# One pool of SBUF slots for raw and split expert weights in a fused attention, MLP and top-1 expert kernel

## The chip, the cores and the metric

The kernel runs on one core of a Trainium2 chip. The metric is the device time of one execution in microseconds: the median of the runs of the kernel before is 708.6 us (three runs, 708.15 to 708.81).

## What is computed

The input is `q`, `k`, `v` of shape (4, 8, 576, 64). Three stages follow each other on 2304 tokens of 512 values:

```python
# 1 attention in a window: query i sees keys i-63 .. i
attn = softmax(where(0 <= i - j < 64, q @ k.T / 8, -1e9)) @ v
# 2 MLP, float64 weights (512 x 2048 and 2048 x 512)
x = relu(attn @ w_in) ** 2 @ w_out
# 3 eight experts, top-1, only for tokens with x @ w_skip > 0
e = argmax(x @ w_gate); gate = softmax(x @ w_gate)[e]
out = x + gate * (relu(x @ w1[e]) @ w2[e])     # w1: 512 x 1024, w2: 1024 x 512
```

All matmuls are float32 in accuracy. Stages 2 and 3 get it by splitting each operand into a rounded high part ("hi", type fp32r) and the rest ("lo"), and adding three products: hi*hi, hi*lo and lo*hi.

## The kernel before

Tokens are worked on in nine chunks of 256 (18 tiles of 128). The MLP walks `units`, pairs of a chunk and one of eight blocks of 256 hidden columns: `l1` (line 428) computes a block's hidden values, `l2` (line 448) two units later adds its part of the output. Attention of the next chunk, the routing of the last one and the preparation of weights are put between them by `inject` (line 596). After the last chunk comes a stage written in a fixed order (from line 705), in which the last two tiles are routed, and then the experts, also in fixed order (from line 872).

An expert takes its tokens in tiles of 128. `static(e, xt)` (line 851) does the first tile of expert e in straight code, `extras(e, ...)` (line 837) the second and further ones, under run-time conditions (lines 839, 842, 844) that every engine tests for itself and jumps over when they are false. In these data expert 0 has two tiles, expert 2 three, every other one at most one, so the order of work is static 0, extra 0, static 1, two extras of 2, static 2, 3, 4, 5, 6, 7, with a jump over the extras between static 2 and 3, 3 and 4, and so on. `ex_block` (line 764) is one tile: 24 matmuls `l1e` (line 774; three passes of four for each half of the hidden columns: x hi with w hi, x hi with w lo, x lo with w hi), relu on ScalarE (779), four transposes (784) and a split into hi (788, ScalarE) and lo (789, VectorE) for each half, 24 matmuls `l2e` (799), the gated sum (821, VectorE) and an indirect store (823, GpSimd). The input of the next block is transposed and split in the middle of it (lines 757 to 762, 672, 673).

The weights of an expert are eight pieces of 128 x 1024 floats (512 KB), four of w1 and four of w2. `ew_start` (line 470) loads a piece on the SyncE queue into one of eight raw buffers: `r0` to `r3` of a pool `wx`, or half of one of the two buffers `xt`, which the MLP has left. It starts nothing when eight pieces are raw. `ew_split` (line 492) turns the oldest raw piece into hi and lo, in tags `s0` to `s31` of the pool `wp`; the MLP's weights lay there before. Piece m of an expert always takes the same two tags, alternating between two sets of sixteen, one for even and one for odd experts. hi is a copy on ScalarE (504), except for piece (2, 2) of experts 2 to 7, which VectorE copies (502). lo is a subtraction on VectorE (506), except for piece (2, 3) of experts 2 to 7, which GpSimd does.

When this happens is written by hand: `ew_plan` (line 590) for the last chunk (fifteen loads, eleven splits), `EWS` (line 41) for the fixed stage (three loads), then `FILLS` (line 49), which gives for six places in a static block the number of splits of the next expert and of loads: 8 and 8 in all. Eight loads stand between extra 0 and expert 1. Each queue works in order, so a load that waits for its buffer holds back the loads behind it.

Of the kernel before, what the change touches and what calls it, by code (L numbers as in the profile page):

```python
# [8 lines left out]
F32 = mybir.dt.float32  # L9
F32R = mybir.dt.float32r  # L10
# [9 lines left out]
P = 128  # L20
B, H, S, D = 4, 8, 576, 64
NTOK = B * S
DM = H * D
NT = NTOK // P
CT = 2
NCH = NT // CT
# [4 lines left out]
NJ = DFF // 256  # L31
NE = 8
POOL_LO = ((2, 3),)
SPLIT_V = 5
DVE_HI = ((2, 2),)
PRO = [int(c) for c in '0010101010']
QK_H = (0, 1)
WARM = 10
NST = 3
LOADN = 3  # L40
EWS = (3, 0, 0)
LATE = (0,)
KEEP = (14, 20, 12, 12)
LOOK = 5
# [1 line left out]
DOT0 = 1  # L46
DOT00 = 6
ROW = NE * NT
FILLS = ((2, 2), (1, 1), (1, 1), (2, 2), (2, 2), (0, 0))
TAIL = 3  # L50
FE = 1024
KF = FE // P
# [9 lines left out]
def body(ctx, tc, qt_d, kt_d, vw_d, wi_d, wo_d, w9_d, w9r_d, w1_d, w2_d, out):  # L62
    nc = tc.nc
# [7 lines left out]
    wp = pool("wp", 1)  # L71
# [92 lines left out]
        if t != 3 * CT - 1 and n < NT:  # L164
            load(n)

    wi_t, wo_t = {}, {}
    raw_q = []
    conv_n = [0]

# [23 lines left out]
    def conv_next():  # L194
        if not raw_q:
            return
        raw, tag, kind, j, half = raw_q.pop(0)
        hw, lw = raw[:, :, 1], raw[:, :, 0]
        f = st.tile([P, 512], I32, tag="f", name="f")
        ff = f.bitcast(F32)  # L200
        hf = hw.bitcast(F32)
        nc.scalar.activation(out=hf, in_=hf, func=AF.Copy, scale=F64_SCALE)
        nc.gpsimd.tensor_scalar(
            out=hf, in0=hf, scalar1=F64_MAX, scalar2=-F64_MAX, op0=ALU.min, op1=ALU.max)
        nc.vector.tensor_scalar(
            out=f, in0=hw, scalar1=3, scalar2=None, op0=ALU.logical_shift_left)
        nc.vector.scalar_tensor_tensor(
            out=f, in0=hw, scalar=SIGN, in1=f, op0=ALU.bitwise_and, op1=ALU.bitwise_or)
        nc.vector.scalar_tensor_tensor(
            out=f, in0=lw, scalar=29, in1=f,  # L210
            op0=ALU.logical_shift_right, op1=ALU.bitwise_or)
        w = wp.tile([P, 2, 512], F32R, tag=tag, name=f"w{kind}{j}_{half}")
        (wi_t if kind == "i" else wo_t)[j, half] = w
        nc.scalar.copy(out=w[:, 0, :], in_=ff)  # L214
        conv_load(nc.gpsimd.tensor_tensor(
            out=w[:, 1, :], in0=ff, in1=w[:, 0, :].bitcast(F32), op=ALU.subtract))
# [125 lines left out]
    def rt_logits(t):  # L342
        xT = x2T_t.pop(t)
        pl = psa()
        for k in range(KD):
            nc.tensor.matmul(
                pl[:, 0:10], lhsT=xT[:, k * P:(k + 1) * P], rhs=w9[:, k, :],
                start=(k == 0), stop=(k == KD - 1))
        lg = small.tile([P, 10], F32, tag="lg", name="lg")
        nc.vector.tensor_copy(out=lg, in_=pl[:, 0:10])  # L350
        rt_argmax(t, lg)
# [110 lines left out]
            x2_evac(c * CT + 1, acc_t[c][1], 1)  # L462

    w1_t, w2_t = {}, {}
    ew_load, ew_raw = [], []
    ew_pool = []

    pair = []

    def ew_start():  # L470
        if not ew_load:
            return
        kind, e, i = ew_load[0]
        if len(ew_raw) > (6 if kind == 2 and i % 2 == 0 else 7):
            return
        ew_load.pop(0)
        r = (8 * e + 4 * (kind - 1) + i) % 8
        if r < 4:
            raw = ew_pool[0].tile([P, 1024], F32, tag=f"r{r}", name=f"r{kind}_{e}_{i}")
        else:  # L480
            if r % 2 == 0:
                pair.append(xtp.tile([P, 2, 1024], F32, tag="xt", name=f"r{kind}_{e}_{i}"))
            raw = pair[-1][:, r % 2, :]
        if kind == 1:
            nc.sync.dma_start(out=raw, in_=w1_d[e, i * P:(i + 1) * P, :])
        else:
            nc.sync.dma_start(  # L487
                out=raw.rearrange("p (a b) -> p a b", b=DM),
                in_=w2_d[e, i * 2 * P:(i + 1) * 2 * P, :].rearrange("(k p) n -> p k n", p=P))
        ew_raw.append((kind, e, i, raw))  # L490

    def ew_split():
        if not ew_raw:
            return
        kind, e, i, raw = ew_raw.pop(0)
        m = 2 * ((8 * e + 4 * (kind - 1) + i) % (2 * NJ))
        hi, lo = [
            wp.tile([P, 1024], F32R, tag=f"s{m + h}", name=f"e{kind}_{e}_{i}_{h}")
            for h in range(2)]
        (w1_t if kind == 1 else w2_t)[e, i] = (hi, lo)  # L500
        if (kind, i) in DVE_HI and e > 1:
            nc.vector.tensor_copy(out=hi, in_=raw)  # L502
        else:
            nc.scalar.copy(out=hi, in_=raw)  # L504
        eng = nc.gpsimd if (kind, i) in POOL_LO and e > 1 else nc.vector
        eng.tensor_tensor(out=lo, in0=raw, in1=hi.bitcast(F32), op=ALU.subtract)  # L506

    def grp_ops(c):
        grp = [(c * CT + i, g) for i in range(CT) for g in range(2)]
# [42 lines left out]
    if True:  # L552
# [34 lines left out]
            for _ in range(PRO[s]):  # L587
                conv_next()

        ew_plan = {(0, 0): 4, (1, 0): 1}  # L590
        for j in range(2, NJ - 1):
            ew_plan[j, 1] = 2

        def inject(u, s):
            for op in slots.pop((u, s), ()):
                op()
            for _ in range(2 if u < 2 else 1):
                conv_next()
            v = u - first[NCH - 1]
            for _ in range(ew_plan.get((v, s), 0)):  # L600
                ew_start()
            for _ in range(ew_plan.get((v - 1, s), 0) if v <= SPLIT_V else 0):
                ew_split()

        n_u = len(units)
        for u in range(n_u):
            if u == first[2]:
                assert not raw_q
                st_stack.close()
                (w9p,), st_stack = scoped(("w9p", 1, {}))  # L610
                w9b = w9p.tile([P, NE + 1, DM], F32, name="w9b")
                nc.sync.dma_start(
                    out=w9b, in_=w9r_d.unsqueeze(0).to_broadcast([P, NE + 1, DM]))
                w9b_t.append(w9b)
            if u == last[1] + LAG + 2:
                ps_s_stack.close()
                ps_a.append(pool("ps_a2", 2, space=PSUM))
            if u == first[NCH - 1]:
                st_stack.close()
                kv_stack.close()  # L620
                (wx, gx), st_stack = scoped(("wx", 1, {}), ("gx", 1, {}))
                ew_pool.append(wx)
                for e in range(NE):
                    ew_load += [(1, e, i) for i in range(4)] + [(2, e, i) for i in range(4)]
            if u < n_u:
                l1(*units[u])
                inject(u, 0)
            if u >= LAG:
                c, j = units[u - LAG]
                if c < NCH - 1 or j < NJ - TAIL:  # L630
                    l2(c, j)
                inject(u, 1)
        c, ta, tb = NCH - 1, NT - 2, NT - 1
        tabs = gx.tile([P, ROW, 2], I32, name="tabs")
# [70 lines left out]
        with tc.manual_schedule():  # L705
# [3 lines left out]
            xa = x2_t[ta]  # L709
            xT0 = ps_acc.tile([P, DM], F32, tag="acc0", name="xT0")  # L710
            l2(c, NJ - TAIL, (1,))
            for _ in range(EWS[0]):
                ew_start()
            rt_tr(ta, 1)
            for j in range(NJ - TAIL + 1, NJ - 1):
                l2(c, j, (1,))
            rt_logits(ta)
            place(xT0, early, ident, True)
            for _ in range(EWS[1]):
                ew_start()  # L720
            l2(c, NJ - 1, (1,), (0,))
            pa = rank_mm(ta)
            sela = slot_of(ta, pa)
            rt_rank(ta, pa)
            rt_scatter(ta)
            l2(c, NJ - 1, (1,), (1,))
            x2_evac(tb, acc_t[c][1], 2)
            xb = x2_t[tb]
            pick_mm(0, sela)
# [21 lines left out]
            nc.vector.tensor_scalar(  # L751
                out=cnt, in0=cnt, scalar1=7, scalar2=None, op0=ALU.logical_shift_right)
            nc.scalar.dma_start(out=tabs, in_=tab_v)
            for _ in range(EWS[2]):
                ew_start()

        def ex_x(tx, inner=True):
            xg = tx[2]
# [91 lines left out]

        def static(e, xt):
            def fill(i):
                n, m = FILLS[i]
                if i == LOADN and e + 1 < NE:
                    for x in range(e + (e > 0), e + 2):
                        load_n(x)
                for _ in range(n):
                    if ew_raw and ew_raw[0][1] <= e + 1:
                        ew_split()
                for _ in range(m if e > 0 else 0):  # L860
                    ew_start()

            if e + 2 < NE:
                t0[e + 2] = fetch(e + 2, 0, 0, e + 2)
            if e + 2 < NE:
                t1[e + 2] = fetch(e + 2, 1, 1, e + 2)
            return ex_block(
                e, t0[e], xt, fill,
                (lambda: ex_x(t0[e + 1], False)) if e + 1 < NE else (lambda: None),
                e in LATE)  # L870

        with tc.manual_schedule():
            t0[1] = fetch(1, 0, 0, 1)
            t1[0] = fetch(0, 1, 1, 0)
            t1[1] = fetch(1, 1, 1, 1)
            xt = static(0, xt)
            extras(0, t1[0])
            for _ in range(8):
                ew_start()
            for e in range(1, NE):  # L880
                extras(e, t1[e])
                xt = static(e, xt)
# [46 lines left out]
```

## Time and profile before

| | |
|---|---|
| median of the runs | 708.6 us |
| span of the profiled execution | 705.2 us; what lies around it isn't listed apart, the three runs lie 3.0 to 3.6 us above the span |
| attention and MLP | to about 541 us |
| static 0 and extra 0 | about 541 to 568 us |
| static 1, two extras of expert 2 | 569.2 to 609.4 us |
| static 2 to 7, ending with the stores | 609.8 to 705.2 us |
| busy share | TensorE 94%, VectorE 69%, ScalarE 44%, GpSimd 23% |

The page of the profile gives the busy share of each engine in 40 equal slices of the span (17.6 us each), and the groups of instructions that cost most. Further views were asked of the trace: which wait of an engine was ended by what, the instructions in order of time, the busy time in chosen stretches with the granted clock of TensorE (1.00 is 2.4 GHz), and all the records of one source line. A wait that ended by "issue" is one for which the trace shows no other engine and no transfer.

### The profile page before, as it was taken

What the parts mean: (1) busy time and instruction counts of PE and PEld (TensorE: products, weight loads), DVE (VectorE), ACT (ScalarE), POOL (GpSimd) and SP (SyncE); (2) the same over time, 40 slices, a digit from 0 to 9 for tenths busy, and PEclk for the clock granted to TensorE, in tenths of its full rate; (3) what the DMA queues carried; (4) which work ended last, traced back from release to release, by engine and by line L of the source; (5) the groups of instructions that cost most, each with busy time, mean ns of one, the idle gap of its engine ahead of it and who ended that gap; (6) DMA issues with size and microseconds to landing.
All of it is one profiled execution on the core that took longest, in us unless ns stands there. A gap on an engine that the chain in (4) does not pass through costs nothing. (4 is left out here: it accounts for less than half of the span.)

```text
span 705.2 us, 12314 instructions
## 1 busy us (share of the span) xinstructions
PE 659.6 (94%) x4461; PEld 571.9 (81%) x4461; DVE 486.3 (69%) x1354; ACT 307.8 (44%) x729; POOL 160.0 (23%) x181
## 2 busy tenths in 40 slices
PE   6699798899999999999999999999999898998786
PEld 4588687679998989989989989889988676776564
DVE  5989999967937836935945945954755363399871
ACT  4775535443434424334334334344442352476541
POOL 5556555510100000000000000030011432226420
PEclk9889999999999999999999999999999999999998
DMA  8964543344123123022122121116335644288820
GB/s 288 265 214 140 166 128 122 113 127 166 35 66 98 38 61 98 31 68 78 51 68 78 51 68 66 62 61 238 122 115 190 218 153 141 73 287 323 284 72 8
DMA packets 51076, 88.70 MB, mean 126 GB/s; under 512 B 24046, under 2 KB 24302, under 8 KB 50864
## 3 DMA queue, kind: packets, MB, share of 16 engines
q1 hardware_dynamic: 47584, 83.38, 35.6%
q0 software_dynamic: 2976, 3.95, 1.7%
q8 instruction: 46, 0.75, 0.4%
q10 hardware_dynamic: 432, 0.32, 0.1%
q14 instruction: 38, 0.31, 0.1%
HBM read 79.07 MB, written 12.49 MB: 130 GB/s over the span
## 5 line engine op out<-in xcount | busy, mean ns | idle before, releaser
L424 PE MATMUL h<-xt,wi 128*128 128x256 f32 x576 | 166.5, 290 | 5.1 <-ACT r L437 3.1
L426 PE MATMUL h<-xt,wi 128*128 128x256 f32 x576 | 165.1, 288 | 0.0
L425 PE MATMUL h<-xt,wi 128*128 128x256 f32 x576 | 164.4, 287 | 0.0
L424 PEld LDWEIGHTS h<-xt,wi 128*128 128x128 f32 x576 | 111.4, 193 | 9.5 <-ACT r L437 4.1
L424 PE MATMUL acc<-wo,gh 128*128 128x512 f32 x288 | 115.7, 406 | 2.5 <-ACT wo L214 2.5
L426 PE MATMUL acc<-wo,gl 128*128 128x512 f32 x288 | 112.7, 393 | 1.4 <-DVE gl L445 1.4
L425 PE MATMUL acc<-wo,gh 128*128 128x512 f32 x288 | 113.6, 394 | 0.0
L425 PEld LDWEIGHTS h<-xt,wi 128*128 128x128 f32 x576 | 111.5, 194 | 2.5
L426 PEld LDWEIGHTS h<-xt,wi 128*128 128x128 f32 x576 | 111.5, 194 | 0.4
L444 DVE TENSOR_TENSOR r<-r 128x512 f32<-128x512 f32 x72 | 53.5, 744 | 62.2 <-ACT gh L443 62.0
L437 ACT ACTIVATE r<-h 128x512 f32<-128x512 f32 x72 | 42.3, 593 | 115.6 <-PE h L426 113.3
L506 DVE TENSOR_TENSOR e<-r,e 128x1024 fp32r<-128x1024 f32 x58 | 73.3, 1283 | 28.0 <-ACT e L504 21.5
L416 POOL DMA_INDIRECT tab_d<-route,posi x18 | 19.5, 1086 | 314.7 <-DVE mx L356 182.5
L335 DVE CUSTOM_DVE_ANT_0 prod<-sm,w9b 128x512 f32<-128x512 f32 x108 | 74.1, 686 | 0.2
L504 ACT CAST e<-r 128x1024 fp32r<-128x1024 f32 x58 | 59.6, 1050 | 27.6 <-PE h L426 14.4
L263 ACT ACTIVATE sm<-sm,nmx 128x128 f32<-128x128 f32 x144 | 56.1, 392 | 26.6 <-DVE nmx L257 25.1
L426 PEld LDWEIGHTS acc<-wo,gl 128*128 128x128 f32 x288 | 54.1, 188 | 13.4 <-DVE gl L445 2.1
L424 PEld LDWEIGHTS acc<-wo,gh 128*128 128x128 f32 x288 | 54.0, 189 | 12.4 <-ACT wo L214 3.4
L774 PE MATMUL h<-e,xh 128*128 128x512 f32 x176 | 49.4, 410 | 13.0 <-issue 6.6
L425 PEld LDWEIGHTS acc<-wo,gh 128*128 128x128 f32 x288 | 54.4, 189 | 8.4
L445 DVE TENSOR_TENSOR gl<-r,gh 128x512 fp32r<-128x512 f32 x72 | 53.3, 741 | 1.9
L774 PEld LDWEIGHTS h<-e,xh 128*128 128x128 f32 x176 | 31.9, 191 | 23.3 <-issue 14.9
(158 smaller groups left out, 1065.0 us busy)
## 6 DMA issues: line engine op xcount, KB each, us to landing
r<-in_w_dram SPq DMA_DIRECT2D x64, 512.0 KB, 5.4
v<-in_vw_dram SPq DMA_DIRECT2D x18, 512.0 KB, 3.6
ri<-in_wi_dram SPq DMA_DIRECT2D x16, 512.0 KB, 4.0
ro<-in_wo_dram SPq DMA_DIRECT2D x16, 512.0 KB, 3.5
k<-in_kt_dram SPq DMA_DIRECT2D x18, 384.0 KB, 3.9
qpad<-in_qt_dram SPq DMA_DIRECT2D x36, 128.0 KB, 3.2
x_d<-sm SPq DMA_DIRECT2D x17, 256.0 KB, 2.6
out_dram<-sm SPq DMA_DIRECT2D x17, 256.0 KB, 3.0
```

The costliest lines, as they stand in the source:

```text
L263: nc.scalar.activation(out=e[:, u, :], in_=e[:, u, :], func=AF.Exp, bias=nmx[:, u:u + 1], scale=-1.0, accum_out=sums[:, u:u + 1])
L335: nc.vector.tensor_tensor_reduce(out=prod, in0=x2_t[t], in1=w9b_t[0][:, j, :], scale=1.0, scalar=0.0, op0=ALU.mult, op1=ALU.add, accum_out ...
L416: nc.gpsimd.indirect_dma_start(out=tab_d, out_offset=bass.IndirectOffsetOnAxis(ap=posi, axis=0), in_=route[:, t, :], in_offset=None, bound ...
L424: nc.tensor.matmul(out_ap, lhsT=ah, rhs=bh, start=start, stop=False)
L425: nc.tensor.matmul(out_ap, lhsT=ah, rhs=bl, start=False, stop=False)
L426: nc.tensor.matmul(out_ap, lhsT=al, rhs=bh, start=False, stop=stop)
L437: nc.scalar.activation(out=r, in_=hp.rearrange("p a b -> p (a b)"), func=AF.Relu)
L444: nc.vector.tensor_tensor(out=r, in0=r, in1=r, op=ALU.mult)
L445: nc.vector.tensor_tensor(out=glf, in0=r, in1=ghf.bitcast(F32), op=ALU.subtract)
L504: nc.scalar.copy(out=hi, in_=raw)
L506: eng.tensor_tensor(out=lo, in0=raw, in1=hi.bitcast(F32), op=ALU.subtract)
L774: nc.tensor.matmul(hp[f], lhsT=xt[a][:, k * P:(k + 1) * P], rhs=w1_t[e, k][b][:, f * 512:(f + 1) * 512], start=(i == 0), stop=(i == len(m1 ...
```

## The change

The two kinds of buffers become one list, `slot_q`, of 40 slots of 128 x 1024 floats: the 32 tags `s0` to `s31`, `r0` to `r3`, and four halves of `xt`. A load takes the first slot of the list (not a half of `xt`, which holds fp32r only), a split takes two and gives back that of its raw piece, and `ew_free` gives back an expert's w1 slots at the fourth place of its static block and its w2 slots at the sixth. `ew_pump(keep)` issues loads as long as more than `keep` slots are free. The MLP's weight tags join the list as the last chunk has used them. `DVE_HI` is empty, so that ScalarE makes every hi. In the last chunk eight pieces are split instead of eleven; static 0 then splits eight where before it split five.

```diff
-SPLIT_V = 5
-DVE_HI = ((2, 2),)
+EWV = (0, 0, 2, 2, 2, 2)
+DVE_HI = ()
-EWS = (3, 0, 0)
-FILLS = ((2, 2), (1, 1), (1, 1), (2, 2), (2, 2), (0, 0))
+FILLS = ((2, 3), (1, 2), (1, 0), (2, 3), (2, 0), (0, 5))
...
-    def ew_start():
...
+    ew_load, ew_raw, slot_q, w_slot = [], [], [], {}
+
+    def slot(dt):
+        n = next(n for n, q in enumerate(slot_q) if dt is F32R or isinstance(q, tuple))
+        q = slot_q.pop(n)
+        if isinstance(q, tuple):
+            return q[0].tile([P, 1024], dt, tag=q[1], name=f"e_{q[1]}"), q
+        return q, q
+
+    def slot_pair():
+        pr = xtp.tile([P, 2, 1024], F32R, tag="xt", name="e_xt")
+        slot_q.extend([pr[:, 0, :], pr[:, 1, :]])
+
+    def ew_pump(keep):
+        while ew_load and len(slot_q) > keep:
+            kind, e, i = ew_load.pop(0)
+            raw, q = slot(F32)
...
+            ew_raw.append((kind, e, i, raw, q))
 
     def ew_split():
...
-        kind, e, i, raw = ew_raw.pop(0)
-        m = 2 * ((8 * e + 4 * (kind - 1) + i) % (2 * NJ))
-        hi, lo = [
-            wp.tile([P, 1024], F32R, tag=f"s{m + h}", name=f"e{kind}_{e}_{i}_{h}")
-            for h in range(2)]
+        kind, e, i, raw, q = ew_raw.pop(0)
+        (hi, qh), (lo, ql) = slot(F32R), slot(F32R)
         (w1_t if kind == 1 else w2_t)[e, i] = (hi, lo)
+        w_slot[kind, e, i] = (qh, ql)
...
         eng.tensor_tensor(out=lo, in0=raw, in1=hi.bitcast(F32), op=ALU.subtract)
+        slot_q.append(q)
+
+    def ew_free(kind, e):
+        for i in range(4):
+            slot_q.extend(w_slot[kind, e, i])
...
             v = u - first[NCH - 1]
-            for _ in range(ew_plan.get((v, s), 0)):
-                ew_start()
-            for _ in range(ew_plan.get((v - 1, s), 0) if v <= SPLIT_V else 0):
-                ew_split()
+            if v >= 0 and s == 1:
+                for _ in range(EWV[v] if v < len(EWV) else 0):
+                    ew_split()
+                ew_pump(3 if v < NJ else NE + 1)
...
             def fill(i):
-                n, m = FILLS[i]
+                n, keep = FILLS[i]
+                if e > 0 and i == 3:
+                    ew_free(1, e)
+                if e > 0 and i == 5:
+                    ew_free(2, e)
...
-                for _ in range(m if e > 0 else 0):
-                    ew_start()
+                if e > 0:
+                    ew_pump(keep)
...
             extras(0, t1[0])
-            for _ in range(8):
-                ew_start()
+            ew_free(1, 0)
+            ew_free(2, 0)
+            ew_pump(5)
```

In the fixed stage the three loads of `EWS` are replaced by `ew_pump(NE + 1)` at four places.

## Rows read from the trace of the kernel before

**Rows 1.** The page: busy share of the DMA engines, 40 slices of 17.6 us.
```profile
DMA  8964543344123123022122121116335644288820
```
**Rows 2.** Waits of TensorE, 609 to 690 us: total, times, longest.
```profile
PE h L774 <- issue: 7.3, 4, 2.8
PE h L774 <- PEq L839: 2.3, 1, 2.3
PE h L774 <- PEq L844: 0.4, 1, 0.4
```
**Rows 3.** TensorE in order of time (start, us): static 1 and 3 to 7.
```profile
569.16 2.08 PE L774 MATMUL h<-e,xh 128*128 128x512 f32 x8 [1.03 <-PEq L839]
...
625.88 0.73 PE L774 MATMUL h<-e,xl 128*128 128x512 f32 x2 [0.73 <-issue]
...
636.45 1.84 PE L774 MATMUL h<-e,xh 128*128 128x512 f32 x7
639.58 0.50 PE L774 MATMUL h<-e,xh 128*128 128x512 f32 x1 [1.29 <-issue]
...
650.85 1.16 PE L774 MATMUL h<-e,xh 128*128 128x512 f32 x4
654.44 1.20 PE L774 MATMUL h<-e,xh 128*128 128x512 f32 x4 [2.44 <-issue]
...
666.40 0.47 PE L774 MATMUL h<-e,xh 128*128 128x512 f32 x1
669.70 2.66 PE L774 MATMUL h<-e,xh 128*128 128x512 f32 x7 [2.83 <-issue]
672.16 1.91 PE L774 MATMUL h<-e,xl 128*128 128x512 f32 x4
...
686.06 2.08 PE L774 MATMUL h<-e,xh 128*128 128x512 f32 x8 [2.30 <-PEq L839]
```
**Rows 4.** TensorE's jump at line 839 after static 2 to 6: ns, start us.
```profile
L839 PEldq COMPARE_BRANCH  x1: 343/343/343, 620.7 to 620.7; - x1
...
L839 PEldq COMPARE_BRANCH  x1: 320/320/320, 634.6 to 634.6; - x1
...
L839 PEldq COMPARE_BRANCH  x1: 322/322/322, 648.9 to 648.9; - x1
...
L839 PEldq COMPARE_BRANCH  x1: 313/313/313, 664.5 to 664.5; - x1
...
L839 PEldq COMPARE_BRANCH  x1: 3884/3884/3884, 682.0 to 682.0; - x1
```
**Rows 5.** Stretches: PE, PEld, DVE, ACT, POOL busy (count), clock, DMA share, GB/s.
```profile
632.00:636.00 4.00, 4.00 (x21) 3.26 (x19) 3.96 (x6) 3.89 (x6) 0.97 (x1) 1.00 1.02 413
...
670.00:680.00 10.00, 10.00 (x44) 7.86 (x43) 6.34 (x6) 5.55 (x8) 2.07 (x1) 0.83 0.37 121
...
678.00:682.00 4.00, 4.00 (x22) 3.33 (x22) 3.71 (x5) 3.81 (x6) 0.10 (x1) 1.00 0.01 2
```
**Rows 6.** Casts and a split, groups by line, 609 to 690 us: busy us, mean ns.
```profile
L504 ACT CAST e<-r 128x1024 fp32r<-128x1024 f32 x33 | 33.8, 1051 | 0.4
...
L506 POOL TENSOR_TENSOR e<-r,e 128x1024 fp32r<-128x1024 f32 x5 | 12.1, 2424 | 15.3 <-ACTq L839 15.2
...
L502 DVE CAST e<-r 128x1024 fp32r<-128x1024 f32 x5 | 9.1, 1827 | 0.0
```
**Rows 7.** Expert 0: loads on SyncE, and the transpose for extra 0.
```profile
546.59 4.50 SPq L487 DMA_DIRECT2D r<-in_w_dram  x4
...
554.46 0.66 PE L761 MATMUL a<-ident,xg 128*128 128x128 f32 x4 [1.15 <-DMA xg<-x_d,tabs]
```
**Rows 8.** All gathers of line 648, issue to landing.
```profile
DMA to landing us min/median/max: 3.6/6.1/6.9
```
**Rows 9.** The waits of ScalarE, 553 to 705 us: the one cast at static 1.
```profile
ACT e L504 <- PEq L842: 4.0, 1, 4.0
```
**Rows 10.** The page, DMA issues: a weight piece, KB, us from issue to landing.
```profile
r<-in_w_dram SPq DMA_DIRECT2D x64, 512.0 KB, 5.4
```

More of the change, by code (lines that the diff above doesn't have):

```diff
@@ L165, in load_next @@
             load(n)
-    wi_t, wo_t = {}, {}
+    wi_t, wo_t, w_tag = {}, {}, {}
     raw_q = []
@@ L211, in conv_next @@
             op0=ALU.logical_shift_right, op1=ALU.bitwise_or)
+        w_tag[kind, j, half] = tag
         w = wp.tile([P, 2, 512], F32R, tag=tag, name=f"w{kind}{j}_{half}")
@@ L464, in body @@
     w1_t, w2_t = {}, {}
-    ew_load, ew_raw = [], []
-    ew_pool = []
-    pair = []
-    def ew_start():
[L471 to L490, printed above, removed]
+    ew_load, ew_raw, slot_q, w_slot = [], [], [], {}
[12 more added lines that the diff above has]
+            raw, q = slot(F32)
+            if kind == 1:
+                nc.sync.dma_start(out=raw, in_=w1_d[e, i * P:(i + 1) * P, :])
+            else:
+                nc.sync.dma_start(
+                    out=raw.rearrange("p (a b) -> p a b", b=DM),
+                    in_=w2_d[e, i * 2 * P:(i + 1) * 2 * P, :].rearrange("(k p) n -> p k n", p=P))
+            ew_raw.append((kind, e, i, raw, q))
     def ew_split():
@@ L588, in body, with w_free @@
                 conv_next()
-        ew_plan = {(0, 0): 4, (1, 0): 1}
-        for j in range(2, NJ - 1):
-            ew_plan[j, 1] = 2
+        def w_free(kind, j):
+            slot_q.extend((wp, w_tag[kind, j, h]) for h in range(2))
         def inject(u, s):
@@ L621, in body @@
                 (wx, gx), st_stack = scoped(("wx", 1, {}), ("gx", 1, {}))
-                ew_pool.append(wx)
+                slot_q.extend((wx, f"r{i}") for i in range(4))
                 for e in range(NE):
@@ L626, in body @@
                 l1(*units[u])
+                c, j = units[u]
+                if c == NCH - 1:
+                    if j == 0:
+                        slot_pair()
+                    w_free("i", j)
+                    if j == NJ - 1:
+                        slot_pair()
                 inject(u, 0)
@@ L631, in body @@
                     l2(c, j)
+                    if c == NCH - 1:
+                        w_free("o", j)
                 inject(u, 1)
@@ L711, in body @@
             l2(c, NJ - TAIL, (1,))
-            for _ in range(EWS[0]):
-                ew_start()
+            w_free("o", NJ - TAIL)
+            ew_pump(NE + 1)
             rt_tr(ta, 1)
@@ L716, in body @@
                 l2(c, j, (1,))
+                w_free("o", j)
             rt_logits(ta)
             place(xT0, early, ident, True)
-            for _ in range(EWS[1]):
-                ew_start()
+            ew_pump(NE + 1)
             l2(c, NJ - 1, (1,), (0,))
@@ L726, in body @@
             l2(c, NJ - 1, (1,), (1,))
+            w_free("o", NJ - 1)
             x2_evac(tb, acc_t[c][1], 2)
@@ L753, in body @@
             nc.scalar.dma_start(out=tabs, in_=tab_v)
-            for _ in range(EWS[2]):
-                ew_start()
+            ew_pump(NE + 1)
         def ex_x(tx, inner=True):
@@ L859, in fill @@
                         ew_split()
-                for _ in range(m if e > 0 else 0):
-                    ew_start()
+                if e > 0:
+                    ew_pump(keep)
             if e + 2 < NE:
@@ L877, in body @@
             extras(0, t1[0])
-            for _ in range(8):
-                ew_start()
+            ew_free(1, 0)
+            ew_free(2, 0)
+            ew_pump(5)
             for e in range(1, NE):
```

## The prediction, made before the changed kernel was built or run

> **What bounds the kernel now.** I read the waits of TensorE first. For the last chunk of the MLP that view is empty, and from 609 to 690 us, six straight expert blocks, its only waits are three kinds that name no other engine and no transfer: 7.3 us ended by "issue" and 2.3 and 0.4 us at a jump [rows 2]. VectorE, ScalarE and the weight loads end none of them. So a lighter VectorE or an earlier load is worth nothing there by itself, and the question is what the 10 us are.
>
> The order of TensorE's work tells [rows 3]. The 2.83 us stop in static 6 comes after one matmul of the block, that of static 5 after four, that of static 4 after seven, that of static 3 after ten (the eight x-hi ones and two of the four x-lo ones), and static 7 can't start at all for 2.30 us. The data those matmuls want differ from case to case; a place that slides by exactly three matmuls per expert is a place in the program. TensorE stops where its instructions end and the next stretch of them has to be brought in after the jump over the extras. The jump itself shows it once: after static 6 it takes 3884 ns, otherwise 313 to 343 [rows 4].
>
> From the jump to the first matmul after the stop, or to the jump's own end for static 7, I get 625.88-620.7 = 5.2 us, 639.58-634.6 = 5.0, 654.44-648.9 = 5.5, 669.70-664.5 = 5.2 and 3.9 us [rows 3, 4]. The four slow ones have weight loads in flight: at the jump of 634.6 the DMA engines are full, 413 GB/s; at that of 682.0 their share is 0.01 [rows 5]. So I read the time as 3.9 us alone and 5.0 to 5.5 beside loads. This is the one way in which the change can reach TensorE in this stage. After the longest stop the clock fell, too: 0.83 granted from 670 to 680, between the 1.2 and 2.4 GHz levels [rows 5]; seven matmuls took 2.66 us and four 1.91, where in static 4 and 5 they took 1.84 and 1.16 [rows 3]. That cost 0.82 + 0.75 = 1.6 us.
>
> **The change, part by part.**
>
> *Casts.* Six copies leave VectorE (the five of the window: 9.1 us, 1.83 each, since a GpSimd subtraction of 2.4 us stands beside most) and ScalarE gets six of 1.05 us [rows 6]. None is behind a wait of TensorE: 0. The new ones run at the end of a block behind ScalarE's other casts; its next urgent work is a relu some 3 us into the following block. Their price with the cover gone would be 1.05 us for each of six blocks, 6 us; their gain is at most zero, as no wait ends on VectorE.
>
> The Trainium skill, "SBUF — State Buffer", section "SBUF: two separate sides", says that VectorE and GpSimd lock each other out of a shared port for a whole instruction, also when VectorE only subtracts two SBUF operands. By that rule the subtraction that remains would still wait for GpSimd, and the removed copies would return only their bare time. The sum is zero by either.
>
> *Loads.* Counting the list through by hand: at the end of the last chunk fifteen pieces are raw or on their way, where before eight were the limit. Nothing is then issued until extra 0 is over, except one piece late in static 0. Twelve come after extra 0, and in static 1 to 4 eight per block: one at the third place, three at the fourth, one at the fifth, three at the sixth. None is left for static 5 and 6. Before, the engines are still at 0.8 in the slices up to 670 us [rows 1]. So the last jumps find no load: static 6 falls from 5.2 to 3.9, -1.3 us. Ahead of the jumps after static 2 to 4 I estimate the loads of the third and fourth place to be issued some 3 us before the jump and, at 5.4 us to land [rows 10], to be in flight for 2 us behind it; those of the fifth and sixth wait for GpSimd's subtraction and for TensorE's end of the block, and come after the fetch. I take half of the time as loaded, 4.6 us: -0.6 of 0.73, -0.4 of 1.29, -0.9 of 2.44 [rows 3]. Bounds: nothing (the instructions come as late as before), and 3.9 everywhere, -0.7, -1.1, -1.6 and -1.3. I take -3.2 in all, 0 to -4.7.
>
> *Clock.* The stop of static 6 then falls to 1.5 us. Stops of 2.44 and 2.30 were not followed by a lower clock in their blocks, that of 2.83 was [rows 3, 5]: -1.6, bounds 0 and -1.6.
>
> *Expert 0.* The transpose for extra 0 waits 1.15 us for its gather, and four loads are issued beside it [rows 7]. Gathers land in 3.6 to 6.9 us [rows 8], and these two stood near the upper end. Without the loads I expect them in time: -1.15. But static 0 splits eight pieces where it split five, and one more cast, 1.05 us [rows 6], stands ahead of ScalarE's copy (line 788) that the second half of the output needs; I estimate that 0.4 of it shows. Sum -0.75, bounds -1.15 and +1.05.
>
> *Expert 1.* Here the change adds. Before, ScalarE's first cast of static 1 waits for the end of extra 0 at TensorE [rows 9], because a buffer used under a condition counts as busy to the end of it. The freed slots of expert 0 are of that kind, so eleven loads start at once at 568 us, on a stretch whose first slices had almost none [rows 1]. Continuing the slide of three matmuls, static 1 meets the end of its instructions after sixteen, 3.7 us after 569.16, and no stop is seen there now. Brought in 1.3 us later it would stop by up to 1.3; I take +0.65, bounds 0 and +2.6 (the jump before it late as well).
>
> *Waits added.* A split now writes into slots just freed. ScalarE's cast at the third place takes the raw slot of the second split of the first place, so it must wait for VectorE's subtraction on it, and ScalarE's relu and TensorE's transposes stand behind. VectorE's two subtractions start after the jump and may be held by GpSimd's 2.4 us [rows 6]. I estimate they end 4.7 us into a block that has no stop, the cast is due at 5.0: 0, at worst 0.7 in each of three blocks. A load that waits for its slot holds only loads on SyncE. SyncE's stores of the MLP's output and its table load come before the crowded part.
>
> Sum: -3.2 - 1.6 - 0.75 + 0.65 = -4.9 on a span of 705.2. The runs lie 3.4 us above that span, and I carry this over: 708.6 - 4.9 = 703.7.
>
> **The rivals.**
>
> *The stops stay (chance 0.21, 708.3).* The place of a jump alone would set the stops, and loads would not. For it: the 3.9 us comes from a jump whose own target was missing, the others from the stretch behind a target, so load is not the only difference between them [rows 4]. Against it: the four with traffic all took over 5 us, and the one without is the shortest. The gather's -0.75 and expert 1 would leave 708 to 709. The Trainium skill, "Runtime: NRT & Kernel Launch", section "Instruction fetch mechanics", states that a taken branch out of the two pages held forces a fetch before execution goes on; that the jump of 3884 ns agrees with. It says nothing of loads beside it, which is this rival.
>
> *The program moves (slower; 711, chance 0.11, and 0.07 the other way, 699).* If TensorE's program ahead of the experts gets longer, every jump lands nearer to the end of its stretch; each matmul less is 0.23 us more (eight took 2.08, one 0.47: 1.61 over seven) in each of static 3 to 5 [rows 3]. At five matmuls the gain is used up: three blocks x 5 x 0.23 = 3.5, and about 1.3 more in static 2 and 6. At seven it is 2 to 3 us slower, 711. TensorE's waits before the experts would need a dozen extra instructions. Against: the change moves none of its matmuls, and waits on weights were covered by later ones. Shorter by as much removes nearly all stops but the last, 699.
>
> *Expert 1 and the new waits take it back (slower; 710, chance 0.07).* +2.6 at static 1 and 0.7 in three blocks is 4.7 against the forecast, and with the clock not recovered 1.6 more. It decides when VectorE's second subtraction of the first place ends later than 5 us into the block.
>
> *Loads too deep or too late* would show as casts waiting for a transfer; with sixteen to nineteen pieces ahead of the split I give it none.
>
> **How the numbers follow.** Forecast 703.7, own range 701 to 706.5, chance 0.54. Rivals: 0.21 stays, 0.11 and 0.07 program moved, 0.07 expert 1 and waits. The range reaches from 700.5 (all fetches at 3.9 us, clock, 1.15: 7.5 us less, 701.1, and a little of the shorter program) to 709.8, leaving out 0.2. What a measurement can tell from no change is 0.2%, 1.4 us. Faster: the forecast, the shorter program and some of the first rival, 0.63; the same: most of the first rival, 0.17; slower: 0.20.
>
> **What would show it.** Right: jumps at the same ten, seven, four, one, none matmuls, with 4.6 and 3.9 us to the next matmul; clock 1.00 from 670 to 680; no loads after about 655; no wait of the transpose for extra 0. Wrong: other places of the stops, 5 us beside idle DMA engines, a stop in static 1 over 1.3 us, or TensorE waiting for ScalarE's relu behind a cast.

## The result, and the profile of the changed kernel

The kernel after takes 713.67 us (median of 4 runs, 712.64 to 714.46), the kernel before 708.38 us beside it: the ratio is 1.0072, 95% interval 1.0054 to 1.0089. The change makes the kernel slower by 5.3 us; the forecast was 4.9 us faster, and 713.7 lies above the range.

The profiled execution of the kernel after has a span of 711.9 us and a time of 713.56 us, so 1.7 us lie around a span. That of the kernel before, with a span of 705.2 us, thus ran some 1.5 us below its median, and the two profiles are 6.7 us apart where the medians are 5.3 apart. The ledger below is that of the profiles.

The waits of TensorE, 609 to 700 us, answer to [rows 2], with the last jump in it too: the kinds are the same, and "issue" has grown from 7.3 to 9.3 us.

```profile
PE h L783 <- issue: 9.3, 4, 3.5
PE h L783 <- PEq L848: 2.2, 2, 2.0
PE h L783 <- PEq L853: 0.4, 1, 0.4
```

TensorE in order of time, static 3 to 7 (as [rows 3]; line 774 is now 783):

```profile
622.80 2.08 PE L783 MATMUL h<-e_s,xh 128*128 128x512 f32 x8
...
627.22 0.99 PE L783 MATMUL h<-e_s,xl 128*128 128x512 f32 x2 [1.89 <-issue]
...
639.28 0.47 PE L783 MATMUL h<-e_xt,xh 128*128 128x512 f32 x1 [0.15 <-PEq L848]
...
643.67 0.50 PE L783 MATMUL h<-e_s,xh 128*128 128x512 f32 x1 [2.55 <-issue]
...
661.13 0.50 PE L783 MATMUL h<-e_xt,xh 128*128 128x512 f32 x1 [3.54 <-issue]
...
676.70 1.88 PE L783 MATMUL h<-e_s,xh 128*128 128x512 f32 x7 [1.29 <-issue]
...
691.21 2.78 PE L783 MATMUL h<-e_s,xh 128*128 128x512 f32 x8 [2.04 <-PEq L848]
```

The jumps that go with them (as [rows 4]; line 839 is now 848), ns and start:

```profile
L848 PEldq COMPARE_BRANCH  x1: 342/342/342, 620.9 to 620.9; - x1
...
L848 PEldq COMPARE_BRANCH  x1: 320/320/320, 637.4 to 637.4; - x1
...
L848 PEldq COMPARE_BRANCH  x1: 323/323/323, 654.5 to 654.5; - x1
...
L848 PEldq COMPARE_BRANCH  x1: 313/313/313, 673.0 to 673.0; - x1
...
L848 PEldq COMPARE_BRANCH  x1: 3624/3624/3624, 687.4 to 687.4; - x1
```

The stops stand at the same five places, but their sizes are others: 1.89, 2.55, 3.54, 1.29 and 2.04 us where [rows 3] had 0.73, 1.29, 2.44, 2.83 and 2.30. From the jump to the next matmul it takes 627.22-620.9 = 6.3, 643.67-637.4 = 6.3, 661.13-654.5 = 6.6 and 676.70-673.0 = 3.7 us, and the last jump itself 3.6. Before, the first three were 5.2, 5.0 and 5.5.

The weight loads on SyncE (start, length, count) around these jumps:

```profile
617.68 0.33 SPq L483 DMA_DIRECT2D e_r<-in_w_dram  x1
619.04 1.41 SPq L485 DMA_DIRECT2D e_s<-in_w_dram  x3
...
633.62 0.33 SPq L483 DMA_DIRECT2D e_s<-in_w_dram  x1
634.63 1.41 SPq L485 DMA_DIRECT2D e_s<-in_w_dram  x3
...
650.85 0.33 SPq L483 DMA_DIRECT2D e_r<-in_w_dram  x1
651.86 0.39 SPq L485 DMA_DIRECT2D e_s<-in_w_dram  x1
652.30 0.46 SPq L485 DMA_DIRECT2D e_r<-in_w_dram  x1
652.85 0.42 SPq L485 DMA_DIRECT2D e_s<-in_w_dram  x1
658.72 0.37 SPq L485 DMA_DIRECT2D e_r<-in_w_dram  x1
```

Four pieces are issued in the last 3.2 to 3.8 us ahead of each of the first three jumps, none of them in the last 0.8 us, and none is issued after 659. In the kernel before, one piece was issued 3.3 us ahead of each of these jumps, and two only 0.6 and 0.2 us ahead:

```profile
620.11 0.90 SPq L487 DMA_DIRECT2D r<-in_w_dram  x2
...
633.92 0.90 SPq L487 DMA_DIRECT2D r<-in_w_dram  x2
...
648.31 0.90 SPq L487 DMA_DIRECT2D r<-in_w_dram  x2
```

Stretches with TensorE's busy time, granted clock, DMA share and GB/s (as [rows 5]):

```profile
620.00:630.00 10.00, 7.96 (x30) 0.88 0.80 266
640.00:650.00 10.00, 7.45 (x28) 0.83 0.88 316
...
654.50:658.80 4.30, 2.94 (x12) 1.00 0.88 310
660.00:670.00 10.00, 8.75 (x34) 0.83 0.22 74
670.00:680.00 10.00, 8.55 (x38) 1.00 0.05 16
...
691.00:695.00 4.00, 3.79 (x11) 0.67 0.08 24
```

The clock fell towards its lower level (1.2 of 2.4 GHz) behind four of the five stops; in the kernel before behind one.

**The ledger.** Static 3 starts at 622.80, 0.17 us later than before. Static 4 starts 2.8, static 5 5.6, static 6 8.5, static 7 5.2 us later, and the end is 6.7 later. The stops together have grown by 1.16 + 1.26 + 1.10 - 1.54 - 0.26 = 1.7 us. The other 6.7 - 0.2 - 1.7 = 4.8 us are matmuls at the lower clock: +1.5, +1.5 and +1.9 us in static 3 to 5, -1.6 in static 6, where the clock no longer falls, and +1.5 in static 7, whose first eight took 2.78 us, at full clock 2.08.

**What the stop is made of.** The parts of the profile on DMA queues name one that I had left unread, "instruction". Asked for tenths of a microsecond, it shows a single packet of 0.02 MB behind each jump. In the kernel after, in the tenths from 625.0, 641.2, 658.8 and 674.0 us (packets, MB, share of the 16 engines):

```profile
q8 instruction: 1, 0.02, 62.1%
...
q8 instruction: 1, 0.02, 62.2%
...
q8 instruction: 1, 0.02, 65.4%
...
q8 instruction: 1, 0.02, 69.1%
```

And in the kernel before, from 623.6, 637.1, 651.9, 667.4 and 683.5 us:

```profile
q8 instruction: 1, 0.02, 60.7%
...
q8 instruction: 1, 0.02, 59.5%
...
q8 instruction: 1, 0.02, 79.7%
...
q8 instruction: 1, 0.02, 58.4%
...
q8 instruction: 1, 0.02, 59.9%
```

So the fetch has two parts:

| jump (us) | jump to packet | packet to next matmul |
|---|---|---|
| after, 620.9 / 637.4 / 654.5 | 4.1 / 3.8 / 4.3 | 2.2 / 2.5 / 2.3 |
| after, 673.0 (no loads) | 1.0 | 2.7 |
| before, 620.7 / 634.6 / 648.9 / 664.5 | 2.9 / 2.5 / 3.0 / 2.9 | 2.3 / 2.5 / 2.5 / 2.3 |
| before, 682.0 (no loads; to the end of the jump) | 1.5 | 2.4 |

The second part hardly changes. The first is longer where weight loads were issued ahead of the jump. The trace shows when the packet moved and not when it was asked for; that it waits behind the loads is read from their bytes. At the jump of 654.5 the sum closes: four pieces issued from 650.85 are 2.10 MB, some 0.70 MB had been moved from 650.5 to the jump (175 GB/s for 4.0 us), and in the 4.3 us until the packet 310 GB/s moved 1.33 MB, nearly the 1.40 that were left. At 637.4 it closes too: of the four pieces issued from 633.62 some 0.8 MB had been moved (205 GB/s for 3.8 us), 1.3 MB were left, and 322 GB/s moved 1.2 MB in the 3.8 us until the packet.

```profile
633.62:637.40 3.78, 3.78 (x23) 1.00 0.60 205
637.40:641.20 3.80, 3.57 (x15) 1.00 0.94 322
```

At 620.9 some 1.5 MB were left (2.10 MB less 177 GB/s for 3.2 us) and 1.4 MB moved (337 GB/s for 4.1 us). In the kernel before, 0.7 to 1.2 MB moved between the four jumps with loads and their packets (270, 403, 392 and 244 GB/s for 2.9, 2.5, 3.0 and 2.9 us), less than the 1.1 to 1.8 MB that had been issued and not moved: the pieces issued 0.6 us or less ahead were not all in front of the packet.

### The profile page after: what moved, and what is told of

Same layout as the page of the kernel before. It is cut to its first block, busy times and chain, and to the rows that moved or that the text cites. A ratio compares the mean times of both kernels' runs of the same rounds, so it can differ in the third digit from the quotient of the medians.

```text
span 711.9 us, 12333 instructions
## 1 busy us (share of the span) xinstructions
PE 664.3 (93%) x4461; PEld 575.3 (81%) x4461; DVE 477.9 (67%) x1348; ACT 313.5 (44%) x735; POOL 158.5 (22%) x181
## 5 line engine op out<-in xcount | busy, mean ns | idle before, releaser
L502 DVE TENSOR_TENSOR e_s<-e_s,e_s 128x1024 fp32r<-128x1024 f32 x34 | 43.2, 1286 | 21.9 <-ACT e_s L500 21.0
L783 PE MATMUL h<-e_s,xh 128*128 128x512 f32 x132 | 42.2, 424 | 7.2 <-issue 3.8
L257 DVE CUSTOM_DVE_ANT_0 sm<-a,mask 128x128 f32<-128x128 f32 x112 | 28.6, 302 | 26.1 <-PE a L245 26.1
L443 ACT ACTIVATE gh<-r 128x512 fp32r<-128x512 f32 x72 | 45.4, 634 | 1.2
```

The costliest lines, as they stand in the source:

```text
L257: nc.vector.tensor_tensor_reduce(out=e[:, u, :], in0=s[:, u * P:(u + 1) * P], in1=mk[:, u % 2 * P:(u % 2 + 1) * P], scale=-1.0 / 8.0, scal ...
L443: nc.scalar.activation(out=ghf, in_=r, func=AF.Square)
L783: nc.tensor.matmul(hp[f], lhsT=xt[a][:, k * P:(k + 1) * P], rhs=w1_t[e, k][b][:, f * 512:(f + 1) * 512], start=(i == 0), stop=(i == len(m1 ...
```

## The experiments

Four theories. F: a stop is the time until TensorE's next instructions have come, less the matmuls still held, and loads issued ahead of the jump lengthen it. W: waits that the change adds cost the time, and the place of the program does not matter. C: the casts moved to ScalarE cost it. P: the place of the jumps, or the clock, sets the stops, whatever is loaded.

### The program moved on, in both kernels

```diff
+        for _ in range(98):
+            nc.tensor.matmul(
+                warm[:, 0:8], lhsT=dummy[:, 0:P], rhs=dummy[:, 0:8], start=True, stop=True)
```

These stand behind the warm-up matmuls of TensorE. In the kernel after:

> Changed kernel with 98 tiny matmuls (8 columns) added to the warm-up at the start, 196 instructions more on TensorE ahead of everything, nothing else. Theory F (the stops of static 3 to 7 are TensorE's program running out after the jump, and weight loads issued just ahead of the jump make the fetch longer): the end of a stretch of instructions now comes 55 to 91 instructions into the blocks, later than the fetch takes, so all five stops (1.9, 2.6, 3.5, 1.3 and 2.0 us) and the slow clock behind them go: 697 to 700 us. Rival W (the stops are waits that the new slots put between ScalarE, VectorE and TensorE, or loads that come late): stops at the same matmuls and sizes, 712 to 714.

In the kernel before:

> Kernel before with the same 98 tiny matmuls at the start. Theory F: its stops (0.7, 1.3, 2.4, 2.8, 2.3 us) and the 1.6 us of slow clock go as well: 697 to 700, within 1.5 us of the changed kernel with the same addition, so that the change itself is worth nothing without the stops. Rival W: unchanged, 708 to 710.

Measured: 701.25 us for the kernel after with them (0.9884, 0.9836 to 0.9932) and 703.76 us for the one before (0.9928, 0.9907 to 0.9949). The stops in static 3 to 7 are gone in both. Each ended above its forecast, since the jump into static 1 now has a long wait: 3.4 us in the kernel after, with a clock of 0.79 from 569 to 585, and 3.8 us in the kernel before.

```profile
PE h L786 <- PEq L851: 3.6, 2, 3.4
```

W falls: no wait of the change was taken out, and 12 us went. That the two kernels would be within 1.5 us of each other was a miss here (2.5); see the last set.

### One hi cast back on VectorE

```diff
-DVE_HI = ()
+DVE_HI = ((2, 2),)
```

> Changed kernel with the hi copy of piece (2, 2) given back to VectorE for experts 2 to 7. Theory F: neither cast is on TensorE's path, 713.7 within 1.5 us. Rival C (ScalarE, with six more casts, holds up the relu): 708 to 710, TensorE waiting less for ScalarE.

Measured: 714.01 us (710.12 to 718.13; 1.0091, 1.0053 to 1.0128). C falls. The width of the runs tells something besides: in the profiled one the stops were 1.88, 2.77, 2.90, 1.40 and 1.93 us, nearly those of the kernel after, but the clock was 1.00 in 620 to 630 and in 690 to 695, where the kernel after had fallen. So a stop of some 2 us is not always followed by a lower clock. The granted clocks of its eight runs agree: in mean over the span, the four slowest (714.94 to 718.13) were granted 0.970 to 0.974, the four fastest 0.978 to 0.984.

### No loads for experts 3 to 7

The split reads the raw pieces of expert 2 again, so experts 3 to 7 compute with its weights.

```diff
+        while ew_load and (ew_load[0][1] > 2 or len(slot_q) > keep):
...
+            if e > 2:
+                ew_raw.append((kind, e, i, raw2[kind, i], None))
+                continue
...
```

> Changed kernel without the weight loads of experts 3 to 7 (they split the raw pieces of expert 2 again; this work is left out), splits and matmuls as they were. Theory F: from the jump to the next matmul or to the jump's end 3.6 to 3.9 us after each of static 2 to 6, in place of 6.3, 6.3, 6.6, 3.7 and 3.6; the stops of static 3, 4 and 5 fall to 0, 0.2 and 0.9 us and the clock stays up behind them: about 703. Rival P (the place in the program alone sets the stops): the stops as in the changed kernel, 711 to 713.

Measured: 702.72 us, a single run. TensorE in order of time:

```profile
651.97 0.50 PE L788 MATMUL h<-e_xt,xh 128*128 128x512 f32 x1 [0.28 <-issue]
...
665.67 0.73 PE L788 MATMUL h<-e_s,xh 128*128 128x512 f32 x2 [1.29 <-issue]
...
680.33 0.47 PE L788 MATMUL h<-e_s,xh 128*128 128x512 f32 x1 [2.19 <-PEq L853]
```

Static 3 and 4 have no wait over 0.2 us left, and static 5 stops for 0.28 us where the kernel after stops for 3.54. From the jumps (648.6, 662.0) it is 3.4 and 3.7 us to the next matmul; the packet came 1.0 us behind each. The clock fell behind the last stop alone (0.83 from 680 to 690). P falls: every jump stands where it stood.

### Half of each piece

The loads of experts 3 to 7 keep their number, order and queue and bring 256 KB each; casts and subtractions read that half twice, so the weights of these experts are others.

```diff
+            if e > 2 and kind == 1:
+                nc.sync.dma_start(out=raw[:, 0:512], in_=w1_d[e, i * P:(i + 1) * P, 0:512])
...
```

> The kernel after, in which the loads of experts 3 to 7 bring only half of each piece (256 KB of 512), and the casts and subtractions read that half twice; the number, order and queue of the loads stay. Theory F by bytes: what lengthens the fetch is the bytes ahead of it, so the jump to the next matmul takes 4.3 to 5.3 us in place of 6.3 to 6.6 ahead of static 3, 4 and 5, time 705 to 709. Theory F by number of transfers: 6.3 to 6.6 stays, 712 to 714. Theory P: 712 to 714 too.

Measured: 702.7 us (0.9924, 0.9898 to 0.9949), below the band of F. No wait in static 3 or 4, and in order of time:

```profile
651.88 0.50 PE L789 MATMUL h<-e_xt,xh 128*128 128x512 f32 x1 [0.88 <-issue]
```

651.88 less the jump's 647.9 is 4.0 us, and ahead of static 4 638.64-634.8 = 3.8 us; the packet came 1.2 us behind the jump of 634.8. The bytes ahead matter; the same number of transfers with half the bytes costs next to nothing.

### The loads held to the end of the block

```diff
-FILLS = ((2, 3), (1, 2), (1, 0), (2, 3), (2, 0), (0, 5))
+FILLS = ((2, 3), (1, 2), (1, 40), (2, 40), (2, 40), (0, 5))
...
-        n = next(n for n, q in enumerate(slot_q) if dt is F32R or isinstance(q, tuple))
+        ok = [n for n, q in enumerate(slot_q) if dt is F32R or isinstance(q, tuple)]
+        n = ok[-1 if last else 0]
...
```

> The kernel after, with its eight loads of a static block held back to the end of the block (raw pieces take the slots that were freed last, so that no load can be issued at the third or fourth place), so that they are issued at or behind TensorE's jump and not in the microseconds ahead of it. Theory F (the stop is the time that TensorE's next instructions take to come, and weight loads issued ahead of the jump lengthen it): from the jump to the first matmul after the stop 5.0 to 5.5 us again ahead of static 3, 4 and 5, stops of about 0.7, 1.3 and 2.4 us in place of 1.89, 2.55 and 3.54, 3.7 to 3.9 us ahead of static 6 and 7, time 705 to 708. Theory P (place of the jump in the program, or the clock, alone): stops as in the kernel after, 712 to 714.

Measured: 706.78 us (704.0 to 709.53; 0.9983, 0.9954 to 1.0011). TensorE in order of time:

```profile
641.10 0.50 PE L784 MATMUL h<-e_s,xh 128*128 128x512 f32 x1 [0.68 <-issue]
...
655.08 0.50 PE L784 MATMUL h<-e_s,xh 128*128 128x512 f32 x1 [1.03 <-issue]
```

Static 3 does not stop at all. The jumps of the other two are at 637.0 and 651.3 us: 4.1 and 3.8 us, less than the 5.0 to 5.5 expected. And the DMA engines were busy at both (stretches, columns as above):

```profile
636.00:638.00 2.00, 2.00 (x10) 1.00 1.03 422
650.00:652.00 2.00, 2.00 (x10) 1.00 0.88 356
```

The loads under way at 637.0 had been issued by 630.4, and the next came at 637.55: the engines are full, but only some 0.6 MB moved ahead of the packet (389 GB/s for 1.6 us), which came 1.6 us behind the jump. So it is not the busy share at the jump that counts, but what has been issued and not yet moved, pieces of the last 0.6 us counting less, as in the kernel before. The clock was 1.00 in each 10 us from 620 to 690. The late loads bring new waits for ScalarE's copy hh, 0.3 us in each of static 2, 3 and 4.

### Every jump at its worst place

The kernel before with fewer of the small matmuls:

```diff
+        for _ in range(14):
```

> The kernel before, with 14 matmuls of 8 columns in TensorE's warm-up, which move its program on by 28 instructions; by the slide of three matmuls per expert every jump into static 3 to 7 should then be one like that of static 7 in the kernel before, whose own target has to be brought in. Theory F: the stops after ten, seven, four and one matmuls are gone, each of the five jumps itself takes 3.6 to 5.5 us and holds up the block by 2.0 to 3.7 us; 712 to 718 in all. Theory P's rival (the time hangs on the matmuls' data or on the loads alone): stops where they were, 708 to 710.

Measured: 719.88 us (1.0200, 1.0139 to 1.0260), over the band. The jumps:

```profile
L842 PEldq COMPARE_BRANCH  x1: 4738/4738/4738, 625.0 to 625.0; - x1
...
L842 PEldq COMPARE_BRANCH  x1: 4545/4545/4545, 642.5 to 642.5; - x1
...
L842 PEldq COMPARE_BRANCH  x1: 4371/4371/4371, 659.7 to 659.7; - x1
...
L842 PEldq COMPARE_BRANCH  x1: 4626/4626/4626, 676.7 to 676.7; - x1
```

The stops within the blocks are gone, and the jumps take it all, as F says. The fifth takes 3.5 us. What the band lacked is static 1, where a stop of 2.71 us came up, and the clock, 0.89 from 625 to 670. Fourteen small matmuls in the warm-up cost 12 us (707.9 us beside it), where 98 gained 5: it is their number, and so the place of the jumps, that counts, and not that they run.

### Another place, and what the change is worth without the fetches

The kernel after with more of them:

```diff
-        for _ in range(98):
+        for _ in range(106):
```

> The kernel after, with 106 matmuls of 8 columns in the warm-up in place of the 98 of the first shift, so that the program lies 16 instructions further on. Theory F: no stop over 1 us in static 3 to 7, as with 98; and the jump into static 1, which had 3.4 us with 98 because the stretch behind it had only just been asked for, now finds it some 1.8 us further on its way: 1.5 us there, and the clock fall of that block (eight matmuls in 3.7 us in place of 2.08) smaller or gone. Time 697 to 701. Rival (the 3.4 us has another cause): 700 to 703 as with 98.

Measured: 699.98 us (0.9900, 0.9855 to 0.9945). All that TensorE waits for from 612 us to the end:

```profile
PE h L786 <- PEq L856: 0.4, 1, 0.4
PE h L786 <- PEq L851: 0.2, 1, 0.2
```

At static 1 the wait is 2.1 us (1.5 expected; the trace puts its end down to a cast of ScalarE here, and to the jump in the second run below, 1.9 us). The packet still comes late, 4.3 us behind the jump of 624.0, but now enough instructions are held to cover it. The same again, the kernel before with the same 106, and both the late loads and the 106:

> The kernel after with 106 small matmuls once more, beside the kernel before with the same ones: 699 to 701 as in the first run, under either theory.

> The kernel before with the same 106 small matmuls. With the stops behind the jumps out of the picture in both, its distance to the kernel after with the same shift is what the change is worth apart from the fetches. Theory F with my step for expert 0 (the transpose for extra 0 no longer waits 1.15 us for its gather, the rest costs nothing): 1 to 2.5 us slower than that kernel, about 701 to 702.5. Rival 1 (casts and shared slots cost something besides): the same as that kernel or faster, 698 to 700. Rival 2 (the change gains elsewhere too): 703 or more.

> The kernel after with the loads held to the end of the block and the 106 small matmuls. Theory F: the shift has already hidden the fetches, so when the loads are issued is worth nothing more: within 1.5 us of the kernel with the shift alone, 699 to 701.5. Rival (loads near the jump cost TensorE time by something other than the fetch): 2 to 5 us faster than the shift alone.

Measured in this order: 700.58 us (0.9886, 0.9857 to 0.9916), 700.96 us (0.9908, 0.9882 to 0.9934) and 703.61 us (0.9940, 0.9918 to 0.9963). With the fetches hidden the kernels before and after can't be told apart: the intervals overlap, so the step of 1 to 2.5 us is not shown. With 98 the two lay 2.5 us apart (701.25 and 703.76, overlapping intervals too), so between nothing and some 2.5 us is open. The trace of the kernel before with 106 does have waits that the kernel after lacks: 1.3 us for a gather and 1.0 us for VectorE's subtraction hl. The late loads are then only harmful: 3.2 us of waits for ScalarE's copies hh, and the distance of 3 us lies outside the 1.5 expected.

The kernel after with 106 small matmuls is the fastest seen, 700.0 and 700.6 us, 7 to 8 us below the kernel before; but with the same shift the kernel before can't be told from it.

## Why the prediction was wrong

- **What bounds the stage**: right. The stops are fetches at places that slide through the program; the matmuls added to the warm-up moved them, and the places after ten, seven, four, one and no matmuls stayed in the kernel after.
- **Loads**: this is the step that failed. It had the loads of the third and fourth place issued some 3 us ahead of the jump, which is what happened (the first of four 3.2 us ahead at 620.9, 3.8 and 3.7 at the others), and took that for a gain: "half of the time as loaded, 4.6 us". 6.3 to 6.6 us were measured. In place of a term that falls with the time that loads share with the fetch, the packet waits for the loads already issued. Issuing four of them 0.8 to 3.8 us ahead, where before two of three had come 0.6 us or less ahead, put more bytes in front of it and not fewer: 1.2 to 1.4 MB moved ahead of the packet, before 0.7 to 1.2. The bounds, "nothing" to -4.7, excluded a loss with no row to do it. The term was -3.2; the stops grew by 1.7.
- **3.9 us alone**: right (3.6 and 3.7, and 3.4 to 3.8 without loads), and with it the term for static 6: -1.5 measured, -1.3 forecast.
- **Clock**: right for static 6 alone. I took its one fall as gone and gave the other blocks none; it fell behind four stops. -1.6 became +4.8, the largest term of the result. That stops of 2.44 and 2.30 us had left the clock alone was read from one execution of the kernel before. It also fell behind the stop of static 7, 2.04 us and thus shorter than the 2.30 before; so the 1.5 us there do not follow from a longer stop, and what decides on a fall at this size stays open.
- **Expert 0**: right in mechanism and size. The transposes for extra 0 wait no more, and from the first matmul of static 0 to that of extra 0 it takes 556.16-541.83 = 14.3 us, where 15.1 were needed: -0.8 for -0.75. The kernel after reaches static 0 1.1 us later, which no step had.
- **Expert 1**: no stop came. Instead TensorE waits 0.8 us for ScalarE there, behind a cast, which the prediction had named as a sign of being wrong, and static 1 takes 584.06-569.34 = 14.7 us, before 582.95-569.16 = 13.8. The first extra block of expert 2 gives the 0.9 us back, where among other things a wait of 0.4 us for VectorE is gone; both blocks together are level with before to 0.1 us. Forecast +0.65 by another mechanism.
- **Casts and Waits added**: right from static 2 on, 0: no wait of TensorE from 609 us on names a cast or a split.
- **The rivals**: none of them was it. "The stops stay" had loads without effect; "the program moves" had the right kind of mechanism, the size of the stop, with the wrong cause. The 711 and 710 us of the slower ones lie near the result without explaining it. The 710 counts the +0.65 of expert 1 twice, since its +2.6 takes that in; the sum is 709.4.
- **The Trainium skill**, "Runtime: NRT & Kernel Launch", section "Instruction fetch mechanics", states that the sequencer uses a DMA queue of its own for its instructions. The trace agrees on the queue, and shows that a queue of its own does not spare the packet the wait: 1.0 to 1.5 us without loads, up to 4.3 behind them.

## What to carry to other kernels

Where TensorE stops with no engine and no transfer named, look for a jump ahead and ask the DMA view for the instruction queue's packet: the time from the jump to it is what loads lengthened here, the time from it to the next matmul stayed at 2.2 to 2.7 us. Issue bulk loads well ahead of a taken jump or behind it, not in the 4 us before, or place the jump so that enough instructions are held behind it. When two versions of a kernel with jumps are compared, move the program of both by a few instructions first: here such a shift made the kernel before 7 us faster or 12 us slower, more than the change itself.

## What had not been expected of the hardware

Instruction packets share the DMA engines with data: the same packet came 1.0 to 1.5 us behind the jump with no loads, 1.6 with full engines and some 0.6 MB in front, and 3.8 to 4.3 behind 1.2 to 1.4 MB of fresh loads. The lower clock after a stop of about 2 us is not certain: stops of 1.88 and 1.93 us passed without it in one kernel, and one of 1.89 brought 0.88 in another that differs by a few casts. Runs of the first spread over 8 us (710.12 to 718.13), the slow ones at the lower granted clock; that its stops near 2 us are the reason is likely and not shown.
